# Sketched attention and multiplicative FFN on one core: all transfers chained in program order, a GpSimd step moved behind three others, and the last store issued whole

## The chip, the core and the metric

The kernel runs on one core of a Trainium2 chip (trn2). The metric is the device time of one execution in microseconds (us); less is better. Engine names are those of the profile: PE is TensorE, DVE is VectorE, ACT is ScalarE, POOL is GpSimd, SP is SyncE, which only issues transfers here. A letter q behind an engine's name (SPq, ACTq) means its queue of issues: an issue is not counted as busy time.

## The reference, cut to what matters

Queries, keys and values have 4 batches, 4 heads, 1088 positions and 32 columns each, in float64. Attention is replaced by a sketch of second degree, and its output goes through a feed-forward block that multiplies two projections.

```python
def phi(x):                                   # 8 x 8 = 64 features of a row
    a = np.einsum('rd,bhsd->bhsr', S1, x)
    b = np.einsum('rd,bhsd->bhsr', S2, x)
    return np.einsum('bhsi,bhsj->bhsij', a, b).reshape(*x.shape[:-1], r * r)
q_p, k_p = (phi(q), phi(k))
kv  = np.einsum('bhsf,bhsd->bhfd', k_p, v)
z   = np.sum(k_p, axis=2)
num = np.einsum('bhsf,bhfd->bhsd', q_p, kv)
den = np.einsum('bhsf,bhf->bhs', q_p, z)[..., None] + 1e-06
x   = (num / den)                              # -> 4352 rows of 128
a, b = x @ w1, x @ w2                          # 128 -> 1024
out  = (a * b @ w3) @ w_out                    # 1024 -> 1024 -> 128
```

The denominators `den` are the delicate part: the kernel keeps their factors split into a high and a low half and sums the products of the halves.

## The kernel before

The work is written as named steps, and one string, `ORDER` (L63 to L117), lists them in the order in which they are traced. Every instruction is then tied to the one before it on its engine (L1544 to L1548), with an edge that orders and makes nobody wait. So each engine's own order is that of `ORDER`. What this chain leaves free before the change is how the transfers of the two issuing queues, SP's and ACT's, stand against each other: an ACT transfer is tied to ACT's last instruction and an SP transfer to SP's.

That order matters because of how completions are counted. The program that comes out counts its transfers on eight semaphores, DMAHW0 to DMAHW7, in turn over all queues together, and every transfer waits, before it is issued, until the one that used its semaphore before it (eight places earlier) has landed. SP is in order, so a transfer that waits holds all the stores behind it.

Steps are named by what they work on. `k0.` to `k3.` are the key batches, `q0.` and `q1.` the two halves of 512 positions of the first query batch, `q2`, `q3`, `q4`, `q6` and `qr` the rest, `w0` to `w10` the conversion of the weights from float64, `f0` to `f7` the product of w3 with w_out, and `g0` to `g7` and `gr` nine groups of output rows (eight of 512 and one of 256) that go through the feed-forward block. `s.` steps prepare the sketch matrices S1 and S2, and `warm` steps are matmuls on zeros that keep PE busy.

Three places matter here.

**The denominators of q0 (L1009 to L1129).** The steps run over the engines in this order:

- On DVE: `q0.sly` (L1036), `q0.C1t` (L1007), the features `q0.phi0` and `q0.phi1` (L1139), `k0.Nr` (L892) between these two, `k1.rest0` (L600), then `q1.sm` (L1068) and `q1.st` (L169).
- On POOL: `q0.sca` (L1040), `q0.p01` (L1107), `s.RC` (L345), `q0.scy` (L1040), `q0.p2` (L1111), `q0.p12` (L1115). `scy` completes the low half, `p01` and `p2` are products of the halves and `p12` is a sum.
- On DVE again: `q0.dn` (L1120) sums the products of `p12`, `q1.sh` (L172), `q0.de` (L1125), `w0.j` (L433), `q0.rc` (L1129, the reciprocals), `q0.xs0` and `q0.xs1` (L1209).
- Then PE turns the result (`q0.xt0`, `q0.xt1`, L1218), ACT copies it (`q0.xT0`, `q0.xT1`, L1222), and the first matmul of the feed-forward block, `g0.0aa` (L1458), reads it. It also needs the first half of the converted weights, which POOL finishes in `w0.a0` (L447).

**`s.RC` (L342 to L345)** copies the arranged sketch matrices S1 and S2 into the table RC, for all four batches, in three copies of 128 x 32 numbers. RC is read by the query parts from `q2` on (L1303); q0 and q1 read RS and Rh.

```python
    @step("s.RC")
    def _():
        for x, i, n in ((0, 0, 2), (0, 2, 3), (1, 0, 0)):
            pool.tensor_copy(RC[:, :, x, i], bview(Sc[:, n], [[0, B], [1, r]]))
```

**The last stores (L1432 to L1442, L1500 to L1514).** A full group is stored by four SP transfers (`g7.st`, L1435). The last group, `gr`, has two tiles of 128 rows: tile 0 is copied out of PSUM by ACT (`gr.oT0`), tile 1 by DVE (`gr.oT1`, both L1508). Tile 1 is stored in two halves of 64 rows (32 KB): the first by SP (`gr.st1`), the second by ACT (`gr.st2`). Tile 0 is stored whole by ACT (`gr.st0`), behind `gr.st2`. The order at the end is `gr.oT0 gr.oT1 gr.st2 gr.st1 gr.st0`.

Of the kernel before, what the change touches and what calls it, by code (L numbers as in the profile page):

```python
# [67 lines left out]
k0.T0 s.Pm q1.max q0.restT k0.T1 q0.rm k0.Ta kr0.kT k0.kT1 warm4 warm3 k0.ab0 q0.A0 k0.ab1 k0.Tb kr0.ab s.Pp k1.load  # L68
k1.loadr k0.Ts q0.C0 k0.abc0 k0.kp0 k0.N0 k0.N1 k1.max warm24 k0.abc1 q0.sma k0.kp1 k1.tr1 k0.Na k0.Nh kr0.abc k1.tr0
q1.l2 k1.g v0.zero v0.load warm2 q0.sta k0.Nb k0.Nl q0.sha q0.C0t k1.kT1 q1.l1 q0.A1 k0.kv0 k0.kv3 k0.Nf q0.C1 k0.kv1  # L70
v0.loadr k0.kv2 kr0.kp q0.smy q0.sla k1.lead0 q0.sty q1.rm kr1.load q0.shy k0.kvr warm21 q0.sca q0.p01 s.RC q0.al
q1.C0 q0.sly q0.C1t k0.kvm q0.phi0 k0.Nr k0.kzt k2.load q0.phi1 k1.kT0 k0.kz q0.pt0 k1.rest0 q1.A0 warm8 q1.sm kr1.tr
q0.pc0 q0.pt1 w0.load q0.x0 q0.pc1 w0.c q1.st q0.scy q0.p2 q0.p12 q1.load q0.dn q0.x1 q1.sh q0.de w0.j q0.rc k1.gram0
q0.xs0 q0.xs1 k1.gram1 k1.gram2 k1.gram3 w0.m q1.sl k1.gram4 warm19 k1.Gm k0.kvc q0.xt0 q1.restT q1.sca k2.max w0.a0
q0.xt1 w0.a1 warm16 q1.p01 q1.scy k1.Gt warm5 warm17 warm6 s.AR q1.al q1.p2 q1.p12 q1.dn w1.c q0.xT0 q1.de g0.0aa
q0.xT1 g0.3a g0.2a kr1.kT g0.2c g0.0ac w1.m g0.3c w2.load s.KS k1.Ga k2.g w1.j g0.3b g0.0ab w1.a0 g0.2b g0.0ba k1.T0
# [36 lines left out]
g4.7o g7.1m g4.oT g6.5m gr.2b g7.4a g6.2b gr.2a g7.4c g7.7a gr.2c gr.2m gr.0b gr.6m g6.2m g7.4m gr.3c g4.st g5.st  # L113
g7.7c g6.0o g6.5o g6.2o g6.6o g6.4o g6.1o g6.3o g6.7o gr.0m g6.oT g7.7b g6.st g7.0o gr.0o0 g7.6o g7.5o gr.3b g1.st
gr.1b g7.4o g2.st g7.2o gr.1m g7.7m gr.3m g7.3o g7.1o g7.7o gr.0o1 gr.6o1 gr.6o0 gr.5o0 g7.oT gr.1o0 gr.5o1 gr.1o1
gr.4o1 gr.3o1 gr.2o1 g7.st gr.7o1 gr.4o0 gr.3o0 gr.2o0 gr.7o0 gr.oT0 gr.oT1 gr.st2 gr.st1 gr.st0 warm25 warm20 warm28
"""  # L117


# [4 lines left out]
def make_steps(ctx, tc, q, k, v, S1, S2, moe_w1, moe_w2, moe_w3, moe_w_out, out):  # L124
    nc = tc.nc
    dve, act, pe, pool, sp = nc.vector, nc.scalar, nc.tensor, nc.gpsimd, nc.sync
    B, H, S, D = q.shape
    r = S1.shape[0]
    DM, DF = moe_w1.shape
# [6 lines left out]
    NT = S // 32  # L136
# [6 lines left out]
    def step(name):  # L143
        def keep(f):
            assert name not in steps, name
            steps[name] = f
            return f
        return keep
# [13 lines left out]
    def sb(tag, shape, dtype=F32, bufs=1, name=None):  # L162
        return place(work, tag, shape, dtype, bufs, name or tag)

    def ps(tag, shape, name):
        return place(psum, tag, shape, F32, 1, name)
# [1270 lines left out]
                             oT[i * 32:(i + 1) * 32, :nT * 32].rearrange("p (T d) -> p T d", d=32))  # L1437
        return dst

    def rest_dst(oT, u, t0=0, n=32):  # L1440
        (sp if u and not t0 else act).dma_start(bass.AP(tensor=out.tensor, offset=(NT - 2 + u + t0 * NT) * DM,
                             ap=[[NT * DM, n], [S * DM, B], [1, DM]]), oT[t0 * B:(t0 + n) * B])  # L1442

    ab_sb, o_ps = {}, {}

    def ffn(g, n, dst):
        for c in range(NC):
            halves = 2 if (g, c) in HALVES else 1
            w = n // halves
            for u in range(halves):  # L1450
                x = {}
                su = "" if halves == 1 else "ab"[u]
                c0 = u * w

                @step(f"g{g}.{c}{su}a")
                def _(c=c, c0=c0, x=x, w=w):
                    x["a"] = ps("h", [128, 512], "a_ps")
                    pe.matmul(x["a"][:, :w], w_of(0, c), xT[g][:, c0:c0 + w], start=True, stop=True)  # L1458

                @step(f"g{g}.{c}{su}c")  # L1460
                def _(x=x, w=w):
                    x["s"] = sb("ffa", [128, 512], bufs=2)
                    act.copy(x["s"][:, :w], x["a"][:, :w])  # L1463

                @step(f"g{g}.{c}{su}b")
                def _(c=c, c0=c0, x=x, w=w):
                    x["b"] = ps("h", [128, 512], "b_ps")
                    pe.matmul(x["b"][:, :w], w_of(1, c), xT[g][:, c0:c0 + w], start=True, stop=True)  # L1468

                @step(f"g{g}.{c}{su}m")  # L1470
                def _(c=c, c0=c0, x=x, u=u, w=w):
                    if u == 0:
                        ab_sb[g, c] = sb("ab", [128, 512])
                    dve.tensor_mul(ab_sb[g, c][:, c0:c0 + w], x["s"][:, :w], x["b"][:, :w])  # L1474

            if g != "r":
                @step(f"g{g}.{c}o")
                def _(c=c):
                    if c == 0:
                        o_ps[g] = ps("out", [128, 512], "ps_o")  # L1480
                    pe.matmul(o_ps[g], w3o[:, c], ab_sb[g, c], start=c == 0, stop=c == NC - 1)  # L1481
            else:
                for u in range(2):
                    @step(f"g{g}.{c}o{u}")
                    def _(c=c, u=u):
                        if c == 0:
                            o_ps[g, u] = ps(("out", "kvz")[u], [128, DM], "ps_or")
                        pe.matmul(o_ps[g, u], ab_sb[g, c][:, u * DM:(u + 1) * DM], w3o[:, c],  # L1488
                                  start=c == 0, stop=c == NC - 1)

        if g != "r":
            oT = {}

            @step(f"g{g}.oT")
            def _():
                oT[0] = sb("oT", [128, 512], bufs=2)
                dve.transpose(oT[0], o_ps[g])  # L1497

            step(f"g{g}.st")(lambda: dst(oT[0]))
        else:  # L1500
            z = {}
            for u in range(2):
                @step(f"g{g}.oT{u}")
                def _(u=u):
                    if u == 0:
                        z["o"] = sb("oT", [128, 512], bufs=2)
                    z[u] = z["o"][:, u * DM:(u + 1) * DM]
                    (dve.tensor_copy if u else act.copy)(z[u], o_ps[g, u])  # L1508

                if u == 0:  # L1510
                    step(f"g{g}.st0")(lambda: dst(z[0], 0))
                else:
                    for i in range(2):
                        step(f"g{g}.st{1 + i}")(lambda i=i: dst(z[1], 1, 16 * i, 16))  # L1514

    for g in range(8):
        b, half = divmod(g, 2)
        if g < 2:
            q_part(g, b, half * 512, 512, "AL"[g])
        elif b < 2:  # L1520
            q_wide(g, b, half * 512, 512, lambda t, g=g: (g, t * 128))
        elif half == 0:
            q_wide(g, b, 0, 1024, lambda t, g=g: (g + t // 2, t % 2 * 256))
        ffn(g, 512, main_dst(b, half * 16, 16))
    q_wide("r", None, 0, 256, lambda t: ("r", t))
    ffn("r", 256, rest_dst)

    for i, n in enumerate(WARM):
# [4 lines left out]
@with_exitstack  # L1533
def kernel(ctx: ExitStack, tc: tile.TileContext, *args: bass.AP):
    nc = tc.nc
    steps = make_steps(ctx, tc, *args)
    traced = nc.cur_bb.bb.instructions
    behind = mybir.DependencyInfo(mybir.DependencyClass.NoSync, mybir.DependencyReason.SCHED_ONLY)
    chained = [e.engine for e in (nc.vector, nc.scalar, nc.tensor, nc.gpsimd, nc.sync)]
    last, seen = {}, len(traced)  # L1540
    for name in ORDER.split():
        steps.pop(name)()
    assert not steps, sorted(steps)
    for ins in traced[seen:]:  # L1544
        if ins.engine in chained:
            if ins.engine in last:
                tc.add_manual_dep(ins, last[ins.engine].name, behind, reason="order")
            last[ins.engine] = ins  # L1548


# [28 lines left out]
```

## Time and profile before

| what | value |
|---|---|
| time, median of 3 runs | 256.16 us (255.9 to 256.43) |
| time of the profiled execution | 255.97 us |
| its span in the trace | 254.2 us |
| mean granted PE clock | 0.995 |
| PE busy | 245.7 us, 97% of the span |
| DVE, ACT, POOL busy | 159.2, 100.3 and 82.3 us |
| transfers | 22.02 MB, mean 87 GB/s |

The span runs from the first to the last instruction of the program on the core; some 1.8 us of the time lie outside it. In a row of a timeline the columns are the start in us from the start of the span, the duration in us, the engine, the line, the operation, what is written and read, and how many instructions the row merges; a bracket gives idle time just before it and what ended it. In a row of waits they are who waited for whom, us in total, how many times, and the longest.

### The profile page before, as it was taken

What the parts mean: (1) busy time and instruction counts of PE and PEld (TensorE: products, weight loads), DVE (VectorE), ACT (ScalarE), POOL (GpSimd) and SP (SyncE); (2) the same over time, 40 slices, a digit from 0 to 9 for tenths busy, and PEclk for the clock granted to TensorE, in tenths of its full rate; (3) what the DMA queues carried; (4) which work ended last, traced back from release to release, by engine and by line L of the source; (5) the groups of instructions that cost most, each with busy time, mean ns of one, the idle gap of its engine ahead of it and who ended that gap; (6) DMA issues with size and microseconds to landing.
All of it is one profiled execution on the core that took longest, in us unless ns stands there. A gap on an engine that the chain in (4) does not pass through costs nothing.

```text
span 254.2 us, 6032 instructions
## 1 busy us (share of the span) xinstructions
PE 245.7 (97%) x2511; PEld 140.1 (55%) x2511; DVE 159.2 (63%) x351; ACT 100.3 (39%) x186; POOL 82.3 (32%) x111
## 2 busy tenths in 40 slices
PE   8899999999999999999999999999999999999990
PEld 6789756456644657576454444444435544554570
DVE  4899898999999969647839584523073144531310
ACT  3757689865665675111522343123202200120000
POOL 3269469476273497983002340000000000000000
PEclk9999999999999999999999999999999999999997
DMA  5679856899599420030200000000020000022532
GB/s 184 182 208 361 251 139 155 228 232 235 144 276 232 92 83 0 3 92 1 41 3 3 0 0 5 0 0 3 0 41 0 3 0 0 0 46 37 83 54 52
DMA packets 31147, 22.02 MB, mean 87 GB/s; under 512 B 21264, under 2 KB 25616, under 8 KB 30992
## 3 DMA queue, kind: packets, MB, share of 16 engines
q1 hardware_dynamic: 30352, 21.02, 33.4%
q10 hardware_dynamic: 768, 0.62, 0.8%
q8 instruction: 20, 0.33, 0.6%
q14 instruction: 7, 0.06, 0.1%
HBM read 19.40 MB, written 2.23 MB: 85 GB/s over the span
## 4 chain that ended last, share of the span: by engine, by line
PE 87%; DVE 5%; DMA 2%; POOL 2%; issue 1%; SPq 1%; DVEq 0%; POOLq 0%
PE a_ps L1458 23%; PE b_ps L1468 23%; PE ps_o L1481 22%; PE ps_w3o L480 6%; PE ps_x L1417 2%; PE ps_g L608 2%; PE ps_ac L1303 2%; DMA qh<-in_q_dram 2%; PE ps_or L1488 1%; PE ps_kv L718 1%; POOL RC L345 1%; PE idle_ps L223 1%; PE ps_ab L676 1%; DVE k_m L182 1%; PE ps_kq L754 0%
## 5 line engine op out<-in xcount | busy, mean ns | idle before, releaser
L1474 DVE TENSOR_TENSOR ab<-ffa,b_ps 128x512 f32<-128x512 f32 (+1 forms) x74 | 45.9, 636 | 44.2 <-PE b_ps L1468 34.7
L1463 ACT COPY ffa<-a_ps 128x512 f32<-128x512 f32 (+1 forms) x74 | 38.6, 556 | 86.6 <-PE a_ps L1458 80.8
L1468 PE MATMUL b_ps<-xT,w 128*128 128x512 f32 (+1 forms) x148 | 67.4, 560 | 0.0
L1458 PE MATMUL a_ps<-xT,w 128*128 128x512 f32 (+1 forms) x148 | 66.8, 561 | 0.0
L1481 PE MATMUL ps_o<-ab,w3o 128*128 128x512 f32 x128 | 60.8, 595 | 0.0
L1468 PEld LDWEIGHTS b_ps<-xT,w 128*128 128x128 f32 x148 | 27.4, 190 | 27.9 <-issue 23.4
L1458 PEld LDWEIGHTS a_ps<-xT,w 128*128 128x128 f32 x148 | 27.1, 190 | 27.6 <-issue 22.1
L1481 PEld LDWEIGHTS ps_o<-ab,w3o 128*128 128x128 f32 x128 | 23.8, 190 | 26.0 <-issue 24.3
L444 POOL TENSOR_TENSOR w3c<-cv_c,cv_m 128x512 int32<-128x512 int32 x16 | 20.3, 1284 | 12.5 <-DVE cv_c L433 8.8
L1497 DVE STREAM_TRANSPOSE oT<-ps_o 128x512 f32<-128x512 f32 x8 | 5.7, 713 | 18.7 <-PE ps_o L1481 18.7
L480 PEld LDWEIGHTS ps_w3o<-wo,w3T 128*128 128x128 f32 x128 | 15.4, 192 | 2.9 <-issue 2.2
L480 PE MATMUL ps_w3o<-wo,w3T 128*128 128x128 f32 x128 | 15.4, 275 | 0.0
L1350 POOL TENSOR_TENSOR s_hl<-s_hl,ay_C 128x256 f32<-128x256 f32 (+2 forms) x4 | 3.2, 794 | 37.1 <-DVE s_hl L1346 25.8
L223 PE MATMUL idle_ps<-zeros 128*128 128x256 bf16 x72 | 12.8, 312 | 1.0 <-DVE zeros L195 1.0
L419 ACT ACTIVATE cv_m<-raw 128x1024 int32<-128x1024 uint32 x11 | 13.0, 1183 | 0.0
L231 ACT ACTIVATE cv_c<-raw 128x1024 f32<-128x1024 f32 x11 | 12.8, 1173 | 0.2 <-DMA raw<-in_moe_w_dram 0.2
L626 POOL TENSOR_TENSOR kp<-kabt 128x1024 f32<-128x1024 f32 x6 | 12.1, 2028 | 1.9 <-DVE kabt L694 1.2
L474 DVE STREAM_TRANSPOSE w3T<-w3c 128x1024 f32<-128x1024 f32 x8 | 9.8, 1224 | 1.0 <-POOL w3c L444 1.0
L223 PEld LDWEIGHTS <-zeros 128*128 128x128 bf16 x72 | 7.7, 110 | 4.0 <-issue 1.3
L1398 POOL TENSOR_TENSOR ph<-s_al,s_bs 128x1024 f32<-128x1024 f32 x2 | 5.1, 2560 | 9.2 <-DVE s_bs L1388 9.2
L1428 ACT COPY xT<-ps_x 128x128 f32<-128x128 f32 (+2 forms) x20 | 4.7, 324 | 8.6 <-PE ps_x L1417 8.6
L608 PE MATMUL ps_g<-kk 128*32 128x64 f32 x288 | 7.8, 224 | 0.3 <-DVE kk L600 0.3
(245 smaller groups left out, 302.5 us busy)
## 6 DMA issues: line engine op xcount, KB each, us to landing
raw<-in_moe_w_dram SPq DMA_DIRECT2D x32, 256.0 KB, 6.2
qh<-in_q_dram SPq DMA_DIRECT2D x4, 544.0 KB, 6.0
raw<-in_moe_w_dram SPq DMA_DIRECT2D x4, 512.0 KB, 7.1
out_dram<-oT SPq DMA_DIRECT2D x32, 64.0 KB, 2.0
k<-in_k_dram SPq DMA_DIRECT2D x3, 512.0 KB, 4.0
v<-in_v_dram SPq DMA_DIRECT2D x2, 512.0 KB, 6.4
raw<-in_moe_w_out_dram SPq DMA_DIRECT2D x1, 1024.0 KB, 8.1
kh<-in_k_dram SPq DMA_DIRECT2D x8, 128.0 KB, 2.5
```

The source lines that it names most:

```text
L223: pe.matmul(t, zeros, bview(zeros, [[0, 2], [1, 128]]), start=True, stop=True)
L231: act.activation(dst, hi.bitcast(F32), ACT.Prelu, scale=2.0 ** -112, alpha=-2.0 ** 32)
L419: act.mul(x["m"], words(0).bitcast(U32), 2.0 ** -29)
L444: pool.tensor_tensor(d, c, m, ALU.add)
L480: pe.matmul(t["o"], w3T[ko][:, c], wo[:, c], start=c == 0, stop=c == NC - 1)
L608: pe.matmul(o[h * D:(h + 1) * D], lhs, rhs, start=start, stop=stop, skip_group_check=True)
L626: eng.tensor_mul(dst, bview(av, [list(av.ap[1]), list(av.ap[2]), [0, r]]), bview(bv, [list(bv.ap[1]), [0, r], list(bv.ap[2])]))
L1458: pe.matmul(x["a"][:, :w], w_of(0, c), xT[g][:, c0:c0 + w], start=True, stop=True)
L1463: act.copy(x["s"][:, :w], x["a"][:, :w])
L1468: pe.matmul(x["b"][:, :w], w_of(1, c), xT[g][:, c0:c0 + w], start=True, stop=True)
L1474: dve.tensor_mul(ab_sb[g, c][:, c0:c0 + w], x["s"][:, :w], x["b"][:, :w])
L1481: pe.matmul(o_ps[g], w3o[:, c], ab_sb[g, c], start=c == 0, stop=c == NC - 1)
```

## The change

1. After the chain along each engine, a second chain runs through all transfers in program order, whichever queue issues them. Its edges are of the same kind as those of the first chain.
2. `s.RC` moves in `ORDER` from between `q0.p01` and `q0.al` to behind `q0.p12`. On POOL it thereby moves past `q0.scy`, `q0.p2` and `q0.p12`, and stands ahead of `w0.a0`.
3. Tile 1 of the last group is stored whole (64 KB) by SP, as `gr.st1`. `gr.st2` goes away, so ACT issues only `gr.st0`.

```diff
-v0.loadr k0.kv2 kr0.kp q0.smy q0.sla k1.lead0 q0.sty q1.rm kr1.load q0.shy k0.kvr warm21 q0.sca q0.p01 s.RC q0.al
+v0.loadr k0.kv2 kr0.kp q0.smy q0.sla k1.lead0 q0.sty q1.rm kr1.load q0.shy k0.kvr warm21 q0.sca q0.p01 q0.al q1.C0
...
-q0.pc0 q0.pt1 w0.load q0.x0 q0.pc1 w0.c q1.st q0.scy q0.p2 q0.p12 q1.load q0.dn q0.x1 q1.sh q0.de w0.j q0.rc k1.gram0
+q0.pt1 w0.load q0.x0 q0.pc1 w0.c q1.st q0.scy q0.p2 q0.p12 s.RC q1.load q0.dn q0.x1 q1.sh q0.de w0.j q0.rc k1.gram0
...
-gr.4o1 gr.3o1 gr.2o1 g7.st gr.7o1 gr.4o0 gr.3o0 gr.2o0 gr.7o0 gr.oT0 gr.oT1 gr.st2 gr.st1 gr.st0 warm25 warm20 warm28
+gr.4o1 gr.3o1 gr.2o1 g7.st gr.7o1 gr.4o0 gr.3o0 gr.2o0 gr.7o0 gr.oT0 gr.oT1 gr.st1 gr.st0 warm25 warm20 warm28
...
-    def rest_dst(oT, u, t0=0, n=32):
-        (sp if u and not t0 else act).dma_start(bass.AP(tensor=out.tensor, offset=(NT - 2 + u + t0 * NT) * DM,
-                             ap=[[NT * DM, n], [S * DM, B], [1, DM]]), oT[t0 * B:(t0 + n) * B])
+    def rest_dst(oT, u):
+        (act, sp)[u].dma_start(bass.AP(tensor=out.tensor, offset=(NT - 2 + u) * DM,
+                                       ap=[[NT * DM, 32], [S * DM, B], [1, DM]]), oT)
...
-                if u == 0:
-                    step(f"g{g}.st0")(lambda: dst(z[0], 0))
-                else:
-                    for i in range(2):
-                        step(f"g{g}.st{1 + i}")(lambda i=i: dst(z[1], 1, 16 * i, 16))
+                step(f"g{g}.st{u}")(lambda u=u: dst(z[u], u))
...
             if ins.engine in last:
                 tc.add_manual_dep(ins, last[ins.engine].name, behind, reason="order")
             last[ins.engine] = ins
+        if isinstance(ins, mybir.InstDMACopy):
+            if "dma" in last:
+                tc.add_manual_dep(ins, last["dma"].name, behind, reason="order")
+            last["dma"] = ins
```

More of the change, by code (lines that the diff above doesn't have):

```diff
@@ L70 @@
 q1.l2 k1.g v0.zero v0.load warm2 q0.sta k0.Nb k0.Nl q0.sha q0.C0t k1.kT1 q1.l1 q0.A1 k0.kv0 k0.kv3 k0.Nf q0.C1 k0.kv1
-v0.loadr k0.kv2 kr0.kp q0.smy q0.sla k1.lead0 q0.sty q1.rm kr1.load q0.shy k0.kvr warm21 q0.sca q0.p01 s.RC q0.al
-q1.C0 q0.sly q0.C1t k0.kvm q0.phi0 k0.Nr k0.kzt k2.load q0.phi1 k1.kT0 k0.kz q0.pt0 k1.rest0 q1.A0 warm8 q1.sm kr1.tr
-q0.pc0 q0.pt1 w0.load q0.x0 q0.pc1 w0.c q1.st q0.scy q0.p2 q0.p12 q1.load q0.dn q0.x1 q1.sh q0.de w0.j q0.rc k1.gram0
+v0.loadr k0.kv2 kr0.kp q0.smy q0.sla k1.lead0 q0.sty q1.rm kr1.load q0.shy k0.kvr warm21 q0.sca q0.p01 q0.al q1.C0
+q0.sly q0.C1t k0.kvm q0.phi0 k0.Nr k0.kzt k2.load q0.phi1 k1.kT0 k0.kz q0.pt0 k1.rest0 q1.A0 warm8 q1.sm kr1.tr q0.pc0
+q0.pt1 w0.load q0.x0 q0.pc1 w0.c q1.st q0.scy q0.p2 q0.p12 s.RC q1.load q0.dn q0.x1 q1.sh q0.de w0.j q0.rc k1.gram0
 q0.xs0 q0.xs1 k1.gram1 k1.gram2 k1.gram3 w0.m q1.sl k1.gram4 warm19 k1.Gm k0.kvc q0.xt0 q1.restT q1.sca k2.max w0.a0
```

## Prediction

> **What bounds the kernel now.** The page comes first: PE is busy in nearly the whole span, so what can be won lies where PE waits or where the end is not PE's.
>
> ```profile
> PE 245.7 (97%) x2511; PEld 140.1 (55%) x2511; DVE 159.2 (63%) x351; ACT 100.3 (39%) x186; POOL 82.3 (32%) x111
> ```
>
> PE's last matmul ends at 247.9 us, 6.2 us before the span's end (254.16). So the end belongs to the stores, and the second view is SP's timeline and list of waits:
>
> ```profile
> SPq L1435 <- DMA out_dram<-oT: 4.7, 2, 4.2
> ```
>
> ```profile
> 245.04 0.32 SPq L1435 DMA_DIRECT2D out_dram<-oT  x1
> ```
>
> ```profile
> 247.70 1.31 ACTq L1441 DMA_DIRECT2D out_dram<-oT  x2
> 249.61 1.62 SPq L1435 DMA_DIRECT2D out_dram<-oT  x3
> 251.32 0.61 SPq L1441 DMA_DIRECT2D out_dram<-oT  x1
> ```
>
> SP issues the first store of g7 at 245.04 and is then silent for 4.2 us, although the tile of all four has been ready since 245.01. It goes on at 249.61. What came in between is ACT's first store, issued at 247.70: it lands 1.9 us later, at 249.6. SP's third store waits in the same way for ACT's second (issued 248.43, landing at 250.35). In the built program's counters g7's second store stands eight places behind `gr.st2` and the third behind `gr.st0`: ACT's two transfers were given places ahead of g1's fourth store, long before their turn in program order. SP's last store, issued at 251.32, lands at 253.21; the span ends 0.95 later.
>
> The third view is the chain of waits at the start (start, duration, what), for PE's list of waits has nothing after 28.15 us (its last is for `xs`, 0.2 us):
>
> ```profile
> 21.13 0.73 POOL s_pr L1107
> 21.85 2.59 POOL RC L345 x3
> 24.45 0.42 POOL s_loy L1040
> ...
> 24.94 0.47 POOL s_pr L1111
> ...
> 25.48 0.47 POOL s_pr L1115
> ...
> 25.97 0.42 DVE s_d L1120
> ```
>
> The three copies of `s.RC` stand in the chain with 2.59 us. They are tiny, so their spread needs a reason:
>
> ```profile
> L345 POOL COPY RC<-Sc x3: 673/759/1334, 21.8 to 23.1; 128x32 f32<-128x32 f32 x3
> ```
>
> Each copy ends just after a DVE instruction with two inputs in SBUF: at 22.47, 23.17 and 24.45, where `phi0`, `phi1` and `k1.rest0` end at 22.40, 23.10 and 24.38. So POOL was held for these and needed about 0.07 us itself. The same shows for the shape that the change exposes:
>
> ```profile
> 19.91 0.92 POOL L1040 TENSOR_TENSOR s_hla<-s_hla,s_bs 128x128 f32<-128x128 f32 x1
> ```
>
> ```profile
> 24.41 0.45 POOL L1040 TENSOR_TENSOR s_loy<-s_loy,ay_C 128x128 f32<-128x128 f32 x1
> ```
>
> Beside DVE's `q1.rm` (two SBUF inputs, ending at 20.51) it took 0.92 us and ended 0.32 after it; beside DVE work on PSUM it took 0.45. Holding goes both ways: DVE's L172, 0.28 elsewhere, took 0.54 at 20.44 and ended 0.15 after POOL.
>
> **The end, step by step.** With one chain over all transfers the counters go in program order. Then g1's fourth store takes DMAHW5, which `gr.st2` has now, g2's take 6, 7, 0 and 1, g7's 2 to 5, `gr.st1` 6 and `gr.st0` 7. Each of g7 and `gr` then waits for a store of g1 or g2; the last of these is issued at 242.06 and lands (2.0 us) by 244.1, ahead of g7's tile: nothing. SP issues g7's four stores from 245.04 at the spacing of g6's (0.32, 0.49, 0.51 and 0.50 plus 0.04 between), until 246.98. `gr.oT1` ends at 247.04, so `gr.st1` goes out at about 247.07 and, at the 1.92 us of the 64 KB store on ACT, lands at 249.0. On ACT `gr.st2` is gone. `gr.oT0` ends at 247.91; `gr.st0` is issued 0.03 later, as SP's store is behind its tile (245.01 to 245.04), instead of at 248.43, and lands at 247.94 + 1.92 = 249.86. That is now the last landing, 0.88 us behind SP's, which is the cover of the larger SP store. With the old 0.95 us behind it, the span ends at 250.81: **-3.35 us**. Up to 0.2 more would go if the last wait to be passed is the last in SP's final list (three short ones follow it now, 0.06 each). The two edits are worth unlike shares: the chain alone would leave ACT's second store at 248.43, -2.86; the whole store adds the other 0.49.
>
> At the start the chain shifts counters too: S1, S2, the two halves of k0 and its rest swap the first five. The transfers eight places on then wait for S1 and S2 (which ACT reads from 3.74 on; `w1.load` is issued at 4.25 and 4.90), for k0's first half (0.75 + 2.9 us; `k2.loadr` goes at 5.37) and, from 11.24 on, for k0's rest and second half (1.52 + 4.1 and 1.23 + 2.9). All are there: nothing. Later places are the same as now.
>
> **The start, step by step.** `s.RC` issues three POOL copies and no transfer; they pass `scy`, `p2` and `p12` on POOL. Were they simply gone, `dn` could start when DVE is free, at 25.17 (end of `q1.st`), and not at 25.97: 0.80 us of DVE's idle time. But now `scy`, `p2` and `p12` meet `phi0`, `phi1` and `rest0`. I take the rows above: whoever waits goes next, and POOL's 128x128 needs 0.32 us after its release.
>
> - `scy` is held by `phi0` until 22.40, ends 22.72. `k0.Nr` (0.04 after it) and `phi1` (0.60) end at 23.36, 0.26 later than now. PE's `pt1` starts at 23.52, so this is covered.
> - `p2`, asked for at 22.80, is held by `phi1`, ends 23.68. `rest0` (1.21) follows, to 24.89; `k1.gram0` on PE starts at 25.84, covered.
> - `p12` is held by `rest0`, ends 25.21. DVE's `q1.sm` and `q1.st` read PSUM and run beside it, to 25.68.
> - `dn` then ends at 26.02, not 26.39: -0.37. `w0.j` needs ACT's `w0.c`, done at 26.09; `dn`, `sh` and `de` bring DVE there at 26.36. So `xs`, `xt`, `xT` and `g0.0aa` all come 0.37 earlier (`g0.0aa` at 29.06). ACT is free for `xT0` at 28.49 (end of `w1.c`), it asks at 28.59; `w0.a0` starts at `w0.m`'s end, 27.19, and is done by 28.6.
> - The copies of RC run from 25.21 beside PSUM and reduce work of DVE, at most 0.28 each (POOL's copy of `four`, 32x128). Even at their old 2.65 they end at 27.86 and `w0.a0` at 29.1, 0.1 late. RC is first read at 46.18.
>
> The lower bound of this cost, most gained, is 0.46: `w1.c` on ACT stops `xT0` there. The upper bound is a loss. If POOL gets ahead of DVE three times and holds it for its full rows (0.45 + 0.46 + 0.46, less the 0.20 that the copies took), `dn` is 1.17 - 0.80 = 0.37 later. I take **-0.37**, nearest to the row of L1040 at 19.91, which shows just this meeting. PE waits for no semaphore after 28.15, so the shift should reach the end whole; if a feeding engine can't come along, it is lost.
>
> The Trainium skill has a rule that speaks against this edit: "SBUF — State Buffer", section "Who interferes with whom", says that a VectorE instruction with two SBUF inputs and a GpSimd instruction reading SBUF exclude each other for a whole instruction, and that the first to issue wins. The trace agrees (0.92 against 0.45 us); without the rule the sum would be -0.46 here instead of -0.37.
>
> **Sum.** -3.35 - 0.37 = -3.72 us from the profiled execution's 255.97 (its span 254.16 and 1.8 outside): 252.25. The median of the runs shown, 256.16, is 0.19 above it; I say **252.3 us**. About 0.2% (0.5 us) is what a measurement here can tell from no change.
>
> **Rivals.**
>
> - *The start's gain is eaten.* POOL goes first each time, and `dn` is as late as now or up to 0.37 later: 255.97 - 3.35 + 0 to 0.37 = 252.6 to 253.0. For it: the two engines alternate tightly, 0.04 us decide who asks first. Against: `phi1` asks before `p2` in my working. Chance 0.30.
> - *The chain doesn't do what it says*, and ACT's transfer keeps an early place. It (landing 249.86) then still holds one of g7's stores; with two or three more issues (0.5 each) `gr.st1` goes out between 250.8 and 251.3 and the end is at 253.7 to 254.2, the time with and without the start's gain 255.1 to 256.0. Against: an edge between transfers fixes the order in which counters are dealt. Chance 0.05.
> - *Slower: the edges between the queues become real waits for landing.* Place: the start, where program order alternates S2 (SP), k0 half (ACT), k0 rest (SP), k0 half (ACT), q0 (SP). S2 is there by 3.74, then 2.9 + 4.1 + 2.9 us of landing: q0's load goes out at 13.6 and not 2.31, and the chain of waits starts with that load. +11.3 - 3.7 gives 263.6. It decides from waits of 3.7 us in all. Against: the same kind of edge ties SP's stores now, issued 0.04 us behind each other while each takes 2.0 to land. Chance 0.04.
>
> Forecast (251.8 to 252.6): 0.61. Range 251.5 to 253.2: below, the 0.2 of the last wait, the bound of 0.46 and the runs' spread of 0.26; above, the first rival and 0.2 from the median; the other two are left out. Faster by over 0.2%: 0.93, with half of the second rival. Within: 0.03. Slower: 0.04.
>
> **What would show it.** SP's waits without a landing of `out_dram`, g7's four stores within 2 us, one ACT store as the last to land, some 3.2 us behind the feed-forward matmuls' end and not 6.6. `dn` without idle time before it, `scy` and `p12` stretched to about 0.9 and 1.4 us, the RC copies short. Wrong would be: POOL's three short with `phi1` and `rest0` stretched (first rival), or another wait in SP's list.

## The result, and the profile after

The changed kernel takes 252.38 us (median of 4 runs, 251.99 to 252.48), the kernel before 256.03 beside it: a ratio of 0.9853, 95% interval 0.9836 to 0.9870, or 3.65 us less. The forecast was 252.3, faster. The profiled execution takes 252.42 us with a span of 250.5.

PE's busy time is as before (before: 245.7 us); the span around it is shorter.

```profile
PE 245.4 (98%) x2511; PEld 139.9 (56%) x2511; DVE 160.0 (64%) x351; ACT 100.2 (40%) x186; POOL 82.0 (33%) x111
```

**The end.** Of SP's list of waits, the one row with a landing of `out_dram` is that of the program's last waits (L1574). The row that held g7's stores by 4.7 us is gone.

```profile
SPq L1574 <- DMA out_dram<-oT: 1.9, 3, 0.8
```

SP's timeline behind 244 us has one unbroken run of stores (start, duration, queue, line, what, how many):

```profile
244.82 1.95 SPq L1435 DMA_DIRECT2D out_dram<-oT  x4
246.87 0.62 SPq L1441 DMA_DIRECT2D out_dram<-oT  x1
```

and ACT's has its copy and its one store right behind it:

```profile
247.42 0.27 ACT L1508 COPY oT<-ps_or 128x128 f32<-128x128 f32 x1 [18.48 <-PE ps_or L1488]
247.72 0.64 ACTq L1441 DMA_DIRECT2D out_dram<-oT  x1
```

`gr.st1` lands at 248.87, `gr.st0` last, at 249.71, and the span ends 0.84 later. From the end of the last output matmul (L1488) to the end of the span it is 3.16 us, where it was 6.59.

**The start.** POOL's timeline from 21 us on: `scy`, `p2` and `p12` are two to three times as long as before (0.45, 0.46 and 0.46 us then), and the three copies of RC take 0.49 us together instead of 2.65.

```profile
21.02 0.73 POOL L1107 TENSOR_TENSOR s_pr<-s_hla,s_hiy 128x256 f32<-128x256 f32 x1 [0.29 <-DVE s_hiy L172]
21.71 0.90 POOL L1040 TENSOR_TENSOR s_loy<-s_loy,ay_C 128x128 f32<-128x128 f32 x1
22.69 0.87 POOL L1111 TENSOR_TENSOR s_pr<-s_al,s_loy 128x128 f32<-128x128 f32 x1
23.64 1.45 POOL L1115 TENSOR_TENSOR s_pr<-s_pr 128x128 f32<-128x128 f32 x1
25.04 0.49 POOL L345 COPY RC<-Sc 128x32 f32<-128x32 f32 x3
```

DVE's timeline beside it: `rest0` took 1.61 where it took 1.36, and `dn` (L1120) follows `q1.st` without idle time before it.

```profile
23.17 1.61 DVE L600 TENSOR_TENSOR kk<-k,kk 128x1152 f32<-128x1152 f32 x1
...
25.14 0.42 DVE L169 SCALAR_TENSOR_TENSOR s_t<-s_g,ps_a 128x256 f32<-128x256 f32 x1
25.48 0.41 DVE L1120 TENSOR_REDUCE s_d<-s_pr 128x32 f32<-128x256 f32 x1
```

The chain of waits of this execution goes through PE alone from 19.37 us on up to `g0.0aa`, where that of before went through POOL's sums and the RC copies:

```profile
24.42 1.79 PE ps_xt L1199 x16
26.21 1.82 PE ps_g L608 x86
28.03 0.22 PE idle_ps L223
28.25 0.44 PE ps_xs L1218 x4
```

So in this execution PE itself was late: DVE's `xs0` and `xs1` were done at 27.60 and 27.93, and PE began to turn them only at 28.09. `g0.0aa` started at 29.19 (29.43 before).

Below, four times are read from each trace. **p01** is the end of `q0.p01` on POOL, the last common point ahead of the change at the start. **g0** is the start of `g0.0aa`. **Middle** runs from g0 to the end of the last output matmul, **tail** from there to the end of the span. Runs differ by some tenths in when the first loads land, so the start is compared as g0 behind p01. The times of g0 behind p01, middle and tail are in us, from the one profiled execution of each kernel.

| kernel | time us, median | ratio to before (95%) | g0 behind p01 | middle | tail |
|---|---|---|---|---|---|
| before | 256.03 | | 7.58 | 218.17 | 6.59 |
| after | 252.38 | 0.9853 (0.9836, 0.9870) | 7.44 | 218.20 | 3.16 |
| after, again (r_after) | 252.22 | 0.9852 (0.9837, 0.9866) | 7.19 | 218.18 | 3.16 |
| after, again (r_after2) | 252.12 | 0.9843 (0.9826, 0.9859) | 7.19 | 218.17 | 3.16 |
| e_chain | 253.13 | 0.9874 (0.9827, 0.9922) | 7.59 | 218.17 | 3.77 |
| e_whole | 255.46 | 0.9972 (0.9950, 0.9994) | 7.58 | 218.18 | 6.10 |
| e_allsp | 252.80 | 0.9863 (0.9822, 0.9904) | 7.58 | 218.18 | 3.10 |
| e_rc | 255.69 | 0.9977 (0.9958, 0.9995) | 7.19 | 218.18 | 6.58 |
| e_norc | 252.52 | 0.9859 (0.9845, 0.9874) | 7.58 | 218.19 | 3.15 |
| e_v0 | 252.41 | 0.9857 (0.9843, 0.9872) | 7.20 | 218.18 | 3.14 |
| e_v0pp | 252.62 | 0.9867 (0.9851, 0.9884) | 7.60 | 218.18 | 3.16 |
| e_xs | 255.75 | 0.9984 (0.9962, 1.0005) | 7.87 | 220.38 | 3.16 |
| e_xsv0 | 255.58 | 0.9979 (0.9962, 0.9996) | 7.76 | 221.75 | 3.15 |
| e_xt | 255.89 | 0.9965 (0.9943, 0.9988) | 7.00 | 222.10 | 3.52 |

The medians of e_whole, e_xs and e_xsv0 include one slow run each, which the ratios leave out; without it they are 255.45, 255.11 and 255.43 us.

### The profile page after: what moved, and what is told of

It reads as the page before. It is cut to its first block, busy times and chain, and to the rows that moved or that the text cites. A ratio compares the mean times of both kernels' runs of the same rounds, so it can differ in the third digit from the quotient of the medians.

```text
span 250.5 us, 6030 instructions
## 1 busy us (share of the span) xinstructions
PE 245.4 (98%) x2511; PEld 139.9 (56%) x2511; DVE 160.0 (64%) x351; ACT 100.2 (40%) x186; POOL 82.0 (33%) x111
## 4 chain that ended last, share of the span: by engine, by line
PE 92%; DVE 3%; DMA 2%; issue 1%; SPq 1%
PE a_ps L1458 24%; PE b_ps L1468 24%; PE ps_o L1481 22%; PE ps_w3o L480 6%; PE ps_g L608 3%; PE ps_x L1417 2%; PE ps_ac L1303 2%; DMA qh<-in_q_dram 2%; PE ps_kv L718 2%; PE ps_or L1488 1%; PE idle_ps L223 1%; PE ps_xt L1199 1%; PE ps_ab L676 1%; DVE k_m L182 1%; PE ps_kq L754 0%
```

## The experiments

### The three edits one by one

**e_chain** is the kernel before with the second chain alone.

```diff
+        if isinstance(ins, mybir.InstDMACopy):
+            if "dma" in last:
+                tc.add_manual_dep(ins, last["dma"].name, behind, reason="order")
+            last["dma"] = ins
```

> The kernel before with the chain over all transfers alone; the last stores stay in three parts and s.RC stays behind p01. Theory (places of ACT's stores): SP is never silent between g7's stores, ACT's two stores go out at 0.1 and 0.8 us behind the last matmul, the second lands last; the span ends 3.6 to 3.8 us behind the last matmul of the output group instead of 6.55, so the time is 2.8 to 2.9 us shorter, about 253.2. Rival (the last stores are slow because two queues share the transfer engines, or because of their split): SP's silence stays and the time is within 0.5 us of before.

Measured: 253.13 us. ACT's two stores stand back to back in its timeline, as one row of two issues:

```profile
247.79 1.31 ACTq L1441 DMA_DIRECT2D out_dram<-oT  x2
```

SP's five go from 245.13 to 247.78 without a gap. The tail is 3.77, so the chain alone takes 2.82 us off it.

**e_whole** is the kernel before with tile 1 of the last group stored whole by SP (`gr.st2` out), without the chain.

```diff
-... gr.oT0 gr.oT1 gr.st2 gr.st1 gr.st0 ...
+... gr.oT0 gr.oT1 gr.st1 gr.st0 ...
```

> The kernel before with the whole last store alone, no chain, s.RC as before. Theory: ACT's single store still has an early place, ahead of g1's fourth store, so that g7's third store waits until it lands (about 2.0 us behind its issue); then g7's fourth and SP's whole store follow and land 2 us later: 0.5 to 0.8 us shorter than before, about 255.4. Rival (the split costs the time): 2 us or more shorter.

Measured: 255.46 us, tail 6.10, so 0.49 less. SP's list of waits and its timeline show that one early place of ACT's is left (a place in the turn of the counters ahead of stores that come first in program order). It holds SP's third store of g7 until ACT's only store (issued at 248.59) has landed at 250.58:

```profile
SPq L1435 <- DMA out_dram<-oT: 4.0, 1, 4.0
```

```profile
245.69 5.76 SPq L1435 DMA_DIRECT2D out_dram<-oT  x4
251.54 0.62 SPq L1441 DMA_DIRECT2D out_dram<-oT  x1
```

**e_allsp** takes ACT out of the end altogether, and leaves the chain out: both last tiles are stored whole by SP.

```diff
-        (sp if u and not t0 else act).dma_start(...)
+        sp.dma_start(...)
```

> The kernel before without the chain, the last two tiles stored whole, both by SP, so that no transfer of another queue can stand between SP's; s.RC as before. Theory: no wait on SP between g7's stores, tile 0's store goes out 0.3 us behind the last matmul as with the chain, the span ends 3.1 to 3.3 us behind that matmul: 3.2 to 3.5 us shorter than before, about 252.7. Rival (the chain is needed for another reason than ACT's places): at most 1 us shorter.

Measured: 252.80 us, tail 3.10, the shortest of all. SP's six stores follow each other:

```profile
245.23 2.04 SPq L1435 DMA_DIRECT2D out_dram<-oT  x4
247.37 1.34 SPq L1441 DMA_DIRECT2D out_dram<-oT  x2
```

With no transfer of another queue at the end there is no early place to be dealt, and no hold. The chain is thus one way to the gain, not its cause: what cost 2.8 us was another queue's late transfer standing ahead in SP's counters.

**e_rc** is the kernel before with `s.RC` moved alone.

```diff
-... q0.sca q0.p01 s.RC q0.al ...
+... q0.sca q0.p01 q0.al ...
-... q1.st q0.scy q0.p2 q0.p12 q1.load ...
+... q1.st q0.scy q0.p2 q0.p12 s.RC q1.load ...
```

> The kernel before with s.RC behind p12 alone, stores and transfers as before. Theory (GpSimd and VectorE hold each other): the sum ends 0.4 us earlier although 2.6 us of copying leave the path, scy, p2 and p12 take about 0.9, 0.9 and 1.45 us, k0.Nr and k1.rest0 are stretched by 0.25 each, the three copies take 0.2 each; the first feed-forward matmul comes 0.1 to 0.4 us earlier, depending on when v0's load lands, and the time is shorter by that, about 255.8. Rival 1 (GpSimd's copies were plain path): 0.8 us or more shorter. Rival 2 (eaten): 0 to 0.4 longer.

Measured: 255.69 us. `scy` takes 0.91 us, `p2` 0.87, `p12` 1.46, `rest0` 1.61, each RC copy 0.21; g0 7.19 behind p01 instead of 7.58: -0.39 us. The tail is that of before. The three parts add up: 2.82 of the chain, 0.61 of the whole store beside it (3.77 to 3.16; 0.49 without the chain) and 0.39 of the move make 3.82; the medians differ from those of before on the same chip by 3.65 (after), 3.93 and 3.95 (the two repeats).

### The start again: whose is it now?

In the first profile of the changed kernel the start had gained only 0.14 behind p01, and PE was in the chain throughout. One theory was that PE, held by the landing of v0, the first transfer of the first value batch (19.23 there, 18.93 before), ate the rest. The rival was that the start is DVE's, and this execution an odd one.

**r_after** is the changed kernel again, **e_norc** the changed kernel with `s.RC` back behind `p01`.

> The changed kernel once more, beside the next ones on the same chip: 252.4, 3.6 shorter than before. Theory: TensorE's first matmuls of k0.kv wait for v0's load, and the first feed-forward matmul moves with that landing.

> The changed kernel with s.RC back behind p01; chain and whole store stay. Theory: the end keeps its gain of 3.4 us and the start loses the 0.2 to 0.4 us: about 252.7, 0.1 to 0.4 longer than the changed kernel, RC copies again at 0.7, 0.8 and 1.3 us. Rival (the move is worth nothing, both differ by chance of landing): the same as the changed kernel within 0.1 us.

Measured: 252.22 and 252.52 us; g0 at 7.19 and 7.58 behind p01. In r_after v0 lands at 18.96 and PE is ready at 27.81. The RC copies of the kernel with the step put back (line, engine, operation, out<-in, how many, shortest/median/longest ns):

```profile
L345 POOL COPY RC<-Sc x3: 677/759/1337, 21.8 to 23.1; 128x32 f32<-128x32 f32 x3
```

So the move is worth 0.39 in the traces with and without the chain (0.37 was forecast). The times differ by 0.30 us, with overlapping intervals.

**e_v0** issues v0's transfer earlier, by putting `q0.restT` ahead of `q1.max` on DVE.

```diff
-k0.T0 s.Pm q1.max q0.restT k0.T1 ...
+k0.T0 s.Pm q0.restT q1.max k0.T1 ...
```

> The changed kernel with q0.restT, the last reader of the buffer into which v0 is loaded, ahead of q1.max on VectorE instead of behind it. Theory (after the change TensorE is held at the start by v0's landing, 0.3 us later in its profile than before, and stays 0.45 us behind what VectorE would allow): v0's load goes out 0.6 us earlier, k0.kv starts by 19.1, the transposes of the result follow VectorE's xs again, and the time is 0.2 to 0.45 us shorter than the changed kernel, about 252.0. Rival 1 (the start is VectorE's as predicted): no change. Rival 2 (the landing is set by the transfers' bandwidth, not by the issue): v0 lands when it does now, no change.

Measured: 252.41 us. v0 lands at 18.08 instead of 18.96 and PE is free for `xt` at 27.69 instead of 27.81, yet g0 stays 7.20 behind p01. The theory of v0 falls for the kernel as such. It holds for the one execution in which v0 landed at 19.23: there `xt` began at 28.09, 0.16 behind `xs1`. So in these traces a landing at 18.08, 18.58 (r_after2, below) or 18.96 costs nothing, and one 0.27 later than the last costs 0.25: the start is DVE's, with PE close behind it.

**e_v0pp** is e_v0 with `p2` and `p12` on DVE, so that two of POOL's three sums don't meet it any more.

```diff
-    ... q0.p01 q0.p12
-    q0.p2 q0.sca q0.scy ...
+    ... q0.p01
+    q0.sca q0.scy ...
```

> As the kernel with q0.restT moved ahead, but p2 and p12 run on VectorE (0.29 us each) and no more on GpSimd. Theory (the two engines hold each other): k1.rest0 is back at 1.36 us from 1.61, only k0.Nr stays stretched by scy, and VectorE's own sum ends 0.3 us later than with GpSimd's help, for 0.58 of new work less 0.25 of holding; the time is 0 to 0.3 us longer than with q0.restT alone. Rival (no holding; rest0's 1.61 has another cause): rest0 stays at 1.6 and the sum comes 0.58 us later.

Measured: 252.62 us, g0 at 7.60. DVE's timeline shows what was saved and what was paid: `rest0` is back at 1.36, but the two sums now stand in DVE's own row.

```profile
23.17 1.36 DVE L600 TENSOR_TENSOR kk<-k,kk 128x1152 f32<-128x1152 f32 x1
...
25.23 0.28 DVE L1111 TENSOR_TENSOR s_pr<-s_al,s_loy 128x128 f32<-128x128 f32 x1
25.55 0.29 DVE L1115 TENSOR_TENSOR s_pr<-s_pr 128x128 f32<-128x128 f32 x1
```

0.25 less and 0.65 more (two sums and the gaps between them, 25.23 to 25.88) come to the 0.40 that g0 lost. POOL is the better place for the sums, although it stretches them to twice and three times their length.

### Three attempts to shorten the start further

**r_after2** was the changed kernel once more, beside the next two; **e_xs** moves `q1.st` and `q1.sh` on DVE behind `q0.xs1`; **e_xsv0** does the same on e_v0.

```diff
-... w0.c q1.st q0.scy q0.p2 q0.p12 s.RC q1.load q0.dn q0.x1 q1.sh q0.de w0.j q0.rc k1.gram0
-q0.xs0 q0.xs1 k1.gram1 ...
+... w0.c q0.scy q0.p2 q0.p12 s.RC q1.load q0.dn q0.x1 q0.de w0.j q0.rc k1.gram0
+q0.xs0 q0.xs1 q1.st q1.sh k1.gram1 ...
```

> The changed kernel again, as the yardstick of the two next to it: 252.2 to 252.4 us, first feed-forward matmul about 7.2 us behind the end of p01, 218.18 us from that matmul to the last output matmul, 3.16 us from there to the span's end.

> The changed kernel with q1.st and q1.sh moved on VectorE behind q0.xs1. Theory: with p12 behind the three copies' old place, VectorE's own work is what is left on the path: dn then starts where p12 ends (25.12 in the profile after), w0.j is held by ScalarE's w0.c (26.1), and xs1 ends at about 27.5 instead of 27.96. TensorE, which the matmuls on v0 keep until 27.8 or later, is the next limit, so the first feed-forward matmul gains 0 to 0.2 us: 252.0 to 252.4. Rival: TensorE is not near, and the gain is the whole 0.33, 251.9 to 252.0. Second rival: the path is still p12 on GpSimd, xs1 ends at 27.96 as before and the time is that of the changed kernel.

> The same with q0.restT ahead of q1.max, so that v0's transfer is issued about 0.6 us earlier and the matmuls on v0 are out of the way. Theory: VectorE's xs1 ends at about 27.5, xT0 waits for ScalarE's w1.c (28.16) alone, and the first feed-forward matmul comes 0.33 earlier than in the changed kernel: 251.9 to 252.0 us, and earlier than in the kernel without the v0 edit. Rival: w0.a0 on GpSimd or q1's later work on VectorE takes the gain back, and the time is that of the changed kernel, 252.2 to 252.4.

Measured: 252.12, 255.75 and 255.58 us. No theory had that. `xs1` does come earlier, as said (27.64 and 27.32, against 27.84 in r_after2), but g0 comes 0.7 and 0.6 us later and the middle is 2.2 and 3.6 longer. PE's list of waits in e_xs behind 28 us has three rows, where the changed kernel has none:

```profile
PE ps_g L608 <- ACT ffa L1463: 1.2, 1, 1.2
PE ps_N L860 <- DVE ab L1474: 0.9, 1, 0.9
PE idle_ps L223 <- DVE s_hl L1088: 0.6, 1, 0.6
```

The last of them is at 28.6 us: a filler matmul (one of the `warm` steps) ahead of `g0.0aa` uses a bank of PSUM (the memory that holds PE's results) that q1's low half (`q1.sl`, L1088) still reads, and `q1.sl` now comes 0.9 later. That alone loses the start's gain (g0 at 7.87). The other two stand at 41.5 and 42.7 us. They make 2.1 of the 2.2 us by which the middle grew, and DVE's timeline in e_xs suggests where they come from:

```profile
37.06 0.18 DVE L169 SCALAR_TENSOR_TENSOR T_t<-T_g,ps_T 32x32 f32<-32x32 f32 x1
37.27 1.28 DVE L172 SCALAR_TENSOR_TENSOR T_p<-T_g,T_t 32x32 f32<-32x32 f32 x1
...
39.01 2.13 DVE L854 TENSOR_TENSOR T_p<-T_p 32x32 f32<-32x32 f32 x1
```

POOL's timeline beside it:

```profile
37.24 1.27 POOL L447 TENSOR_TENSOR w<-w,cv_m 128x512 int32<-128x512 int32 x1
38.47 2.63 POOL L600 TENSOR_TENSOR kk<-k,kk 128x1152 f32<-128x1152 f32 x1
```

and in r_after2 the same DVE row, and the POOL row beside it:

```profile
36.34 0.18 DVE L172 SCALAR_TENSOR_TENSOR T_p<-T_g,T_t 32x32 f32<-32x32 f32 x1
```

```profile
36.42 1.27 POOL L447 TENSOR_TENSOR w<-w,cv_m 128x512 int32<-128x512 int32 x1
```

A DVE step that takes 0.18 us in r_after2, with two inputs in SBUF, takes 1.28 here: POOL's L447 began 0.03 us ahead of it, and it ends 0.04 behind POOL. DVE's L854 then ends 0.04 behind POOL's next step, L600, and takes 2.13; in r_after2 it takes 0.76 and ends 0.04 behind L447. In r_after2 DVE was first, by 0.08 us (36.34 against 36.42). So 2.5 us of DVE's time (1.10 and 1.37) hang on who comes first at one place 8 us behind the edit.

All 14 traces of this case fall on the same two sides. In eleven DVE's L172 starts first, by 0.07 to 0.09 us (by 0.35 in the first profile of the changed kernel), and takes 0.18 us (0.43 in that one, where it ends 0.04 behind POOL's step before, L1139). In three, e_xs, e_xsv0 and e_xt below, POOL starts first by 0.03 or 0.04, and it takes 1.27 or 1.28. That PE's two waits follow from this is not shown by itself: no kernel changes this meeting alone.

**e_xt** leaves DVE's and POOL's order as it is. ACT's first copy `xT0` waits in the changed kernel for all four matmuls of `xt`, since both halves lie in one PSUM tile. Here each half has its own, and three fillers in front of `g0.0aa` are gone (which changes how long PE is kept busy, and no result). The lines below leave out those that use the new tiles, and a change of the table that gives each tile its PSUM bank.

```diff
-                    if u == 0:
-                        s["xp"] = ps("t", [128, 512], "ps_xs")[:, :n]
+                    s["xp", u] = ps("t", [128, 512], "ps_xs")[:, :n]
...
-WARM = [16, 10, 6] + [4] * 2 + [2] * 8 + [1] * 16
+WARM = [16, 10, 6] + [4] * 2 + [1] + [0] + [2] * 6 + [1] * 16
```

> The changed kernel with the two halves of q0's turned result in two PSUM tiles instead of one, so that ScalarE's first copy xT0 waits for the first half's matmuls alone, and with three filler matmuls fewer between them and the first feed-forward matmul. In the changed kernel xT0 starts when the fourth matmul of xt ends (28.38, where the second ended at 28.01 and ScalarE was free at 28.05), and the feed-forward block starts 0.47 later, behind six fillers. Theory: only the start is shortened, nothing behind it waits, and the stretch from the first feed-forward matmul to the last output matmul stays at 218.18; g0.0aa starts at 6.86 instead of 7.19 us behind the end of p01, and the time is 251.8 to 252.0 us against 252.1 to 252.4 of the changed kernel. Rival: TensorE comes too early for what VectorE and GpSimd feed it at 33 to 41 us, waits there for what it gained, and the stretch grows by 0.3: 252.1 to 252.4. Second rival, as with q1.st and q1.sh behind xs1: an engine shifted by tenths meets GpSimd's long steps the other way round, TensorE waits for 1 us or more, and the time is 253 to 256.

Measured: 255.89 us, the second rival. `xT0` starts at 28.32, ahead of the last matmul of `xt`, and g0 is at 7.00 behind p01, 0.19 earlier. Then T_p (L172) starts at 36.62, POOL's L447 at 36.58: 1.27 us again, and 2.15 for L854. PE waits 1.0 and 1.2 us at the same two places as in e_xs. One of the 12 runs took 252.87 us. It has no trace; it would fit if DVE was first in it, which is not shown. No kernel tried here beats the changed one by more than the runs' spread.

## Why the prediction was right

Point by point, by its own steps:

- **The hold at the end.** The chain deals the counters in program order, and g7's four stores and `gr.st1` follow each other with nothing between. Forecast for the chain alone -2.86, measured -2.82; for the whole store on top of it -0.49, measured -0.61 (and -0.49 without the chain); together -3.35 with up to 0.2 more, measured -3.43. `gr.st0` was to be the last to land: it is, 1.99 us after its issue (1.92 taken). The span ends 0.84 later. The prediction took 0.95, which runs to DVE's last instruction; to the end of the span, 254.19, it was 1.00. The 0.16 saved is the "up to 0.2 more": SP's wait for this landing is now the last in its list. e_allsp shows that the reason given, ACT's early places, is the right one.
- **The start transfers' shifted counters** were costed at nothing. e_chain has g0 at 7.59 behind p01, as before: nothing.
- **The start.** `scy`, `p2` and `p12` were to take 0.92, 0.88 and about 1.45: 0.90, 0.87 and 1.45. The copies of RC were to be short: 0.20 each. -0.37 was forecast, -0.39 measured in e_rc and between e_norc and r_after. In the first profile of the changed kernel it was less (-0.14), for v0 landed late and PE was not ready; the step had no term for PE. That PE would be ready was not worked out, and in the other traces of the move it was so by little.
- The forecast's rule from the Trainium skill ("SBUF — State Buffer", "Who interferes with whom") is borne out in both directions. POOL's `p12` takes 1.45 us behind DVE's `rest0` and 0.46 elsewhere, and in e_xs DVE waits out two whole POOL instructions. With `p2` and `p12` off POOL, DVE's `rest0` goes from 1.61 back to 1.36.
- **The shift reaches the end whole.** The middle is 218.17 to 218.20 us in all kernels in which DVE starts L172 ahead of POOL's L447, whatever g0 is.
- **The rivals.** The start's gain was not eaten by POOL; the chain did what it says; no edge became a wait for landing. The rival that was not seen is the one of e_xs and e_xt: a shift of tenths turning round a meeting of DVE and POOL at 36 us. In the changed kernel DVE is first there by 0.35 us in the first profile and by 0.08 in r_after and r_after2 (0.09 before). That it would stay first was not worked out, only assumed with "the shift should reach the end whole". On this point the forecast was lucky.

The sum was 252.25 from a profiled execution of 255.97; the three sets of runs have medians of 252.38, 252.22 and 252.12.

## What to carry to other kernels

When an in-order queue falls silent although its data is ready, look at which transfer used its completion counter before, and on which queue that one stands: the cure is the order in which the counters are dealt, or one queue for all. Where two engines hold each other up, as DVE and POOL do here, a change is costed by who asks first, for whole instructions. The same question has to be put at every later meeting that the edit shifts: here the kernels in which POOL was first by 0.03 or 0.04 us have a middle that is 2.2 us longer, and 3.6 to 3.9 longer where PE's clock fell as well. A step that its engine stretches to three times its length can still be in the better place.

## What was not expected of the hardware

PE's clock (the granted clock is the share of full speed that the profile shows for PE). In e_xsv0 PE waited 0.9 and 1.2 us near 42 us, and the granted clock then fell to half. The windows of one microsecond (first and last us, length, busy time of PE, PEld, DVE, ACT and POOL, granted clock, DMA share, GB/s):

```profile
42.00:43.00 1.00, 0.31 (x16) 0.22 (x16) 0.97 (x3) 0.91 (x3) 1.00 (x2) 1.00 0.00 0
43.00:44.00 1.00, 0.40 (x20) 0.43 (x23) 0.93 (x4) 1.00 (x2) 1.00 (x1) 0.75 0.03 8
44.00:45.00 1.00, 1.00 (x64) 1.00 (x60) 1.00 (x2) 1.00 (x4) 0.59 (x1) 0.50 0.00 0
45.00:46.00 1.00, 1.00 (x65) 1.00 (x59) 0.78 (x4) 1.00 (x3) 0.00 (x0) 0.50 0.06 16
46.00:47.00 1.00, 1.00 (x42) 0.94 (x32) 0.00 (x0) 1.00 (x2) 0.00 (x0) 0.54 0.00 0
```

If the clock is either whole or half, 0.75, 0.50, 0.50 and 0.54 are 0.5 + 1 + 1 + 0.92 = 3.4 us at half, or 1.7 us of work lost. In e_xt the clock from 44 to 48 us is 0.66, 0.50, 0.50 and 0.64, which makes 3.4 us again. In the profiled execution of e_xs the same two waits left the clock at 1.00. The runs of e_xs part in the same way, though only one has a trace: six took 254.8 to 255.1 us with a mean clock of 1.0, and five 256.4 to 256.7 with 0.993. The Trainium skill, "TensorE: Matmul & The Clock Gate", section "Part 1: The HAM clock gate (the "warmup" mystery)", has the clock switch between full and half speed by a free-running window of about 3.4 us; the 3.4 us here agree, and a window that runs free would explain why the same waits cost the clock in one run and not in the next, which no run here can show.

Before the change the clock was 0.995 over the span and 0.82 in the window of 245 to 255 us, where PE is mostly idle; after it the mean is 1.00. So what fell there fell in the tail, and the middle is the same 218.2 us.
